# Triangular diagonal score pieces for columns 1 and 2 of the first batch, scored first and completed by DMA transposes

## Chip, cores and metric

One core of one Trainium2 chip. The metric is device microseconds of one execution. The kernel before takes 1192.81 us (median of 3 runs, 1192.8 to 1194.91). On one core the runs have no slow and fast dies to compare.

## The reference, cut to what matters

```python
def _attn_ref(u, v, z):                      # 8 batches, 3008 rows, d_model 256, d_qk 64
    scores = (1.0 / S) * np.matmul(z, z.transpose(0, 2, 1))
    attn = np.maximum(scores, 0.0) ** 2      # symmetric: attn[i, j] == attn[j, i]
    return (u * np.matmul(attn, v)).astype(np.float32)

def _moe_ref(x, w_in, w_out):                # on the 24064 rows of the result
    h = x @ w_in                             # d_ff = 2048
    return ((h * np.cos(h)) @ w_out).astype(np.float32)
```

The attention matrix is symmetric. The kernel uses this: it scores only one side of each pair of pieces and makes the other with a DMA transpose.

## The kernel before

The 3008 rows of a batch are cut into six columns of 512 (the last has 448). A "piece" (b, J, I) holds the squared relu of the scores of key group I against column J, as four blocks of 128 keys. It is made by two score groups, h = 0 and 1: two matmuls on PE, one relu on ScalarE (ACT), one square on VectorE (DVE). 18 buffers hold pieces. In "slot" s = 6 b + J column J is multiplied by v, while the score groups of a later column are put between the matmuls.

```python
    groups = [
        (b, J, I, h)
        for b in range(B)
        for J in range(NC)
        for I in range(0 if b == 0 and J < 3 else J, NC)
        for h in range(2)
    ]
    direct = {(0, 0, 1), (0, 0, 2), (0, 1, 2)}
    # ... cut ...
    def emit_score(later=None):
        b, J, I, h = groups[done_groups[0]]
        done_groups[0] += 1
        cut = I == J and not (b == 0 and J < 3)
        W = 2 * P if cut and h == 0 else width(J)
        # ... cut: two matmuls into e, the second and first half of the rows;
        #     with cut, block n of the diagonal gets (n + 1) * 128 columns only
        nc.scalar.activation(r[:, :, 0:W], e[:, :, 0:W], AF.Relu)
        # ... cut: square r into the piece on VectorE; note the piece for a turn

    def emit_turns(due, more=0):             # on the SP queue, in program order
        # ... cut ...
            if I == J:                       # lower triangle -> upper, three turns
                for rr in range(1, 4):
                    nc.sync.dma_start_transpose(
                        a4[:, 0:rr, rr * P:rr * P + rows],
                        a[0:rows, rr * CW:rr * CW + rr * P],
                    )
            else:                            # one long turn, 16 blocks, to a new piece
                nc.sync.dma_start_transpose(d.rearrange("p (n j) -> p n j", j=P), a)
```

The first three slots have no earlier slot to prepare their pieces, so they are packed by hand:

```python
    def phase_a_first(s, n, extra={}):       # slots 0, 1, 2
        run = 1 if s == 0 else 2
        steps = [                            # dh: the half of the output; k: block of keys
            (dh, k)
            for I in range(0, NC, run)
            for dh in range(2)
            for k in range(4 * I, min(4 * (I + run), last))
        ] + [(2, last)]
        lo, hi = 5 if s == 0 else 2, 42      # n score groups spread over steps lo to hi
        # ...
        for i, (dh, k) in enumerate(steps):
            # ... two value matmuls for step i ...
            for _ in range(at.get(i, 0)):
                emit_score(later=squares if s == 0 and i == lo else None)

    phase_a_first(0, 12, {4: lambda: turn_late(4), 8: lambda: turn_late(5)})
    phase_a_first(1, 12)
    nc.gpsimd.dma_start(w_out16, moe_w_out.rearrange("(k p) f -> p k f", p=P))
    for i in range(2):
        emit_h(0, i)()
    phase_a_first(2, 14)
```

So slots 1 and 2 first read key group 0 at steps 0 to 3, group 1 at steps 4 to 7, and group 2 from step 16.

## Time and profile before

| | before |
|---|---|
| time, median of 3 | 1192.81 us |
| span of the profiled run | 1191.2 us |
| PE (TensorE) busy | 1183.7 us, 99% |
| DVE, ACT, POOL busy | 85%, 67%, 57% |
| mean granted clock | 1.000 |

A busy line gives time, share of the span and instructions of each engine. A timeline line gives start, length, engine, line, operation, and in brackets the idle time ahead of it with what ended it. "PE M L266 <- DVE" in a list of waits means that PE at line 266 waited for DVE.

### The profile page before, as it was taken

Reading aid. Unit: us, or ns where it says so; the run is one execution under the profiler, and the core shown is the slowest. Engines: PE = TensorE matmul, PEld = TensorE weight load, DVE = VectorE, ACT = ScalarE, POOL = GpSimd, SP = SyncE. Lnnn points to the kernel's source line nnn. Section 1 sums busy time; section 2 is a strip of 40 time slices with the busy share of each in tenths; the row PEclk is TensorE's granted clock in tenths of the full one; section 3 lists DMA queues with packets and bytes.
Section 4 is the critical chain, followed back from the end, with each engine's and each line's share of the span. In section 5 each row is a group of like instructions: output and inputs, shape, how many; then the busy total and the mean of one; then the engine's idle time right before and its main releaser. Section 6 shows DMA issues by size and latency. Waiting matters only on the chain.

```text
span 1191.2 us, 29044 instructions
## 1 busy us (share of the span) xinstructions
PE 1183.7 (99%) x11887; PEld 726.8 (61%) x11887; DVE 1011.5 (85%) x1302; ACT 794.9 (67%) x927; POOL 679.0 (57%) x717
## 2 busy tenths in 40 slices
PE   9999999999999999999999999999999999999998
PEld 4556665665566656666566665656666566665566
DVE  6888888889988898888988889888888888888776
ACT  7966676667666676667676676666766666666454
POOL 3286745657466573755647556476555655545452
PEclk9999999999999999999999999999999999999999
DMA  9999999569995799955999469984798837974301
GB/s 160 175 172 158 115 171 130 102 122 104 173 127 101 123 137 166 126 89 103 155 152 130 86 106 158 168 123 70 120 162 152 122 72 120 173 122 84 65 20 54
DMA packets 449142, 148.00 MB, mean 124 GB/s; under 512 B 401264, under 2 KB 432496, under 8 KB 449008
## 3 DMA queue, kind: packets, MB, share of 16 engines
q1 hardware_dynamic: 368464, 112.93, 56.6%
q0 software_dynamic: 80032, 32.78, 27.7%
q8 instruction: 93, 1.52, 0.5%
q10 hardware_dynamic: 512, 0.43, 0.1%
q14 instruction: 41, 0.34, 0.1%
HBM read 66.32 MB, written 24.64 MB: 76 GB/s over the span
## 4 chain that ended last, share of the span: by engine, by line
PE 98%; ACT 1%; DVE 1%; issue 0%; POOL 0%; DVEq 0%; ACTq 0%
PE E L412 27%; PE M L490 23%; PE M L266 20%; PE E L266 19%; PE E L202 6%; PE M L533 1%; ACT r L212 1%; PE M L468 1%; DVE g L423 0%; PE E L673 0%; DVE sm L278 0%; PE E L533 0%; POOL s L441 0%; PE M L696 0%; ACT c L420 0%
## 5 line engine op out<-in xcount | busy, mean ns | idle before, releaser
L420 ACT ACTIVATE c<-E 128x1024 f16<-128x1024 f32 (+1 forms) x384 | 385.7, 1007 | 216.4 <-PE E L412 214.1
L423 DVE SCALAR_TENSOR_TENSOR g<-E,c 128x1024 f16<-128x1024 f32 (+1 forms) x384 | 458.9, 1197 | 62.0 <-ACT c L420 60.9
L212 ACT ACTIVATE r<-E 128x512 f16<-128x512 f32 (+1 forms) x342 | 328.0, 967 | 112.3 <-PE E L202 106.6
L266 PEld LDWEIGHTS <-v 64*128 64x128 f16 x4512 | 245.7, 94 | 229.6 <-issue 18.8
L412 PE MATMUL E<-x,w_in 128*128 128x512 f16 (+1 forms) x1408 | 354.0, 375 | 0.0
L441 POOL TENSOR_TENSOR s<-g 128x512 f16<-128x512 f16 (+1 forms) x184 | 207.8, 1130 | 189.3 <-DVE g L423 139.4
L266 PE MATMUL M<-A,v 64*128 64x512 f16 (+1 forms) x2256 | 283.0, 372 | 0.0
L266 PE MATMUL E<-A,v 64*128 64x512 f16 (+1 forms) x2256 | 278.0, 371 | 0.0
L442 POOL TENSOR_TENSOR g<-g 128x512 f16<-128x512 f16 (+1 forms) x184 | 219.0, 1190 | 14.4
L412 PEld LDWEIGHTS <-w_in 128*128 128x128 f16 x1536 | 133.1, 98 | 108.9 <-issue 19.5
L490 PEld LDWEIGHTS <-g 128*128 128x128 f16 x2816 | 172.5, 98 | 40.8
L217 DVE TENSOR_TENSOR A<-r 128x1024 f16<-128x1024 f16 x240 | 173.2, 734 | 15.1 <-ACT r L212 14.3
L294 POOL TENSOR_TENSOR x<-sm,uT 128x512 f16<-128x512 f32 (+1 forms) x43 | 48.6, 1131 | 223.5 <-DVE sm L278 223.5
L490 PEld LDWEIGHTS <-s 128*128 128x128 f16 x2112 | 129.4, 98 | 32.1 <-DVE s L448 0.5
L202 PE MATMUL E<-zT 64*128 64x512 f16 (+4 forms) x684 | 128.0, 356 | 1.6 <-DVE sm L278 0.7
L448 DVE TENSOR_TENSOR s<-s,g 128x1024 f16<-128x1024 f16 (+1 forms) x92 | 99.7, 1085 | 2.1 <-POOL s L441 2.1
L490 PE MATMUL M<-w_mix,s 128*128 128x128 f16 x1408 | 94.0, 219 | 0.3 <-POOL s L441 0.3
L490 PE MATMUL M<-w_mix,g 128*128 128x128 f16 x1408 | 93.6, 219 | 0.0
L490 PE MATMUL M<-w_out,g 128*128 128x128 f16 x1408 | 93.6, 219 | 0.0
L220 DVE TENSOR_TENSOR A<-r 128x512 f16<-128x512 f16 (+1 forms) x102 | 80.1, 785 | 8.6 <-ACT r L212 7.6
L202 PEld LDWEIGHTS <-zT 64*128 64x128 f16 x684 | 38.7, 94 | 38.4 <-issue 3.8
L450 DVE TENSOR_TENSOR s<-g,s 128x1024 f16<-128x1024 f16 (+1 forms) x92 | 60.6, 661 | 0.0
(58 smaller groups left out, 636.3 us busy)
## 6 DMA issues: line engine op xcount, KB each, us to landing
out_dram<-o SPq DMA_DIRECT2D x87, 256.0 KB, 2.1
v<-in_v_dram POOLq DMA_DIRECT2D x40, 256.0 KB, 11.5
u<-in_u_dram POOLq DMA_DIRECT2D x40, 256.0 KB, 4.5
A<-A SPq DMA_TRANSPOSE x252, 5.3
z<-in_z_dram POOLq DMA_DIRECT2D x14, 192.0 KB, 10.9
z<-in_z_dram POOLq DMA_DIRECT2D x14, 176.0 KB, 6.8
v<-in_v_dram POOLq DMA_DIRECT2D x8, 192.0 KB, 16.1
u<-in_u_dram POOLq DMA_DIRECT2D x8, 192.0 KB, 3.7
```

The source lines that it names most:

```text
L202: nc.tensor.matmul(e[:, t, 0:Wt], zT[rows, k * P:(k + 1) * P], zT[rows, J * CW:J * CW + Wt], start=True, stop=True,)
L212: nc.scalar.activation(r[:, :, 0:W], e[:, :, 0:W], AF.Relu)
L217: nc.vector.tensor_tensor(a4, r4, r4, ALU.mult)
L220: nc.vector.tensor_tensor(a4, r[:, :, 0:W], r[:, :, 0:W], ALU.mult)
L266: nc.tensor.matmul(bank[:, 0:width(J)], vs[b, k // 4][t * H:(t + 1) * H, k % 4, dh * P:(dh + 1) * P], value_rhs(b, J, k, t), start=start, ...
L412: nc.tensor.matmul(e[:, f, 0:W], w_in16[:, k, ft * P:(ft + 1) * P], x[:, k, 0:W], start=(k == 0), stop=(k == 1),)
L420: nc.scalar.activation(c[:, :, 0:W], e[:, :, 0:W], AF.Sin, bias=half_pi, scale=inv_s2)
L423: return lambda: nc.vector.scalar_tensor_tensor(gs[m][:, 2 * i:2 * i + 2, 0:W], e[:, :, 0:W], 1.0, c[:, :, 0:W], ALU.mult, ALU.mult)
L441: nc.gpsimd.tensor_tensor(s1[:, f, 0:n], g[:, f, low], g[:, lower, low], ALU.add)
L442: nc.gpsimd.tensor_tensor(g[:, f, low], g[:, f, up], g[:, f, low], ALU.subtract)
L448: nc.vector.tensor_tensor(s2[:, f, 0:n], s1[:, f, 0:n], g[:, f, up], ALU.subtract)
L490: nc.tensor.matmul(acc[:, k * P:(k + 1) * P], left[:, ft, k * P:(k + 1) * P], right[:, ft, :], start=(ft == 0 and k == 0), stop=(ft == F - ...
```

## The change

The intent: the diagonal pieces (0,1,1) and (0,2,2) are symmetric too, so their upper half need not be scored. This saves work on PE, ACT and DVE in the stretch where ACT has no gaps. The missing blocks come by three transposes each, as everywhere else in the kernel; to give these time to land, the diagonal groups are scored first in their column.

```diff
+    def keys_of(b, J):
+        first = 0 if b == 0 and J < 3 else J
+        return sorted(range(first, NC), key=lambda I: (I != J, I))
+
     groups = [
-        (b, J, I, h)
-        for b in range(B)
-        for J in range(NC)
-        for I in range(0 if b == 0 and J < 3 else J, NC)
-        for h in range(2)
+        (b, J, I, h) for b in range(B) for J in range(NC) for I in keys_of(b, J) for h in range(2)
     ]
@@ emit_score
-        cut = I == J and not (b == 0 and J < 3)
+        cut = I == J and (b > 0 or J > 0)
@@ phase_a_first
                 emit_score(later=squares if s == 0 and i == lo else None)
+                if s < 2:
+                    emit_turns((0, s + 1))
```

## The prediction

> **What bounds the kernel now.** I read the page first: busy shares, then the chain of work that ended last.
>
> ```profile
> PE 1183.7 (99%) x11887; PEld 726.8 (61%) x11887; DVE 1011.5 (85%) x1302; ACT 794.9 (67%) x927; POOL 679.0 (57%) x717
> ...
> PE 98%; ACT 1%; DVE 1%; issue 0%; POOL 0%; DVEq 0%; ACTq 0%
> ```
>
> TensorE (PE) is busy for all but 7.5 us and is 98% of the chain, so nearly anything that keeps PE from its next matmul is paid one for one, and only what shortens PE's own work, or one of its rare waits, is won. An average hides where the change sits, so I went to the place. The diff touches batch 0 alone: two diagonal pieces (0,1,1) and (0,2,2), written (batch, column, key group), scored while the columns ("slots") 0, 1 and 2 are multiplied by v. By the timeline of PE these slots are roughly 9 to 23, 23 to 36 and 38 to 53 us. A table of busy time by windows over 16 to 54 us gives ScalarE (ACT) 36.3 of 38 us, far over its average of 67%, and the timeline of ACT shows slot 0 without a gap:
>
> ```profile
> 13.50 9.60 ACT L212 ACTIVATE r<-E 128x1024 f16<-128x1024 f32 x10
> ```
>
> So in slot 0 ACT sets the pace, PE almost equals it; from 25 us on the chain in order of time is PE again, except around 36 to 41 us, where it passes the copies, cosines and gate of the slot change. That is what makes a triangular cut attractive here. Now PE at the start of slot 1, then at the start of slot 2 (start, length, engine, line, operation; in brackets the idle time before and its releaser):
>
> ```profile
> 23.37 0.40 PE L202 MATMUL E<-zT 64*128 64x512 f16 x2
> 23.58 0.83 PE L266 MATMUL E<-A,v 64*128 64x512 f16 x6
> 25.07 0.39 PE L202 MATMUL E<-zT 64*128 64x512 f16 x2 [0.66 <-DVE sm L278]
> ...
> 39.88 0.39 PE L202 MATMUL E<-zT 64*128 64x512 f16 x2 [0.42 <-DVE g L423]
> 40.09 0.82 PE L266 MATMUL M<-A,v 64*128 64x512 f16 x6
> 41.01 0.39 PE L202 MATMUL E<-zT 64*128 64x512 f16 x2
> 41.22 0.61 PE L266 MATMUL M<-A,v 64*128 64x512 f16 x4
> ```
>
> One "step" of the code is two matmuls of L266; a score group is the two of L202. Each pair's record lasts 0.39 us but the next pair starts 0.22 us later: 0.22 us is its price. Counting steps from a slot's start, 23.58 is steps 3, 4 and 5 of slot 1 and 40.09 is steps 3, 4 and 5 of slot 2; 41.22 is its step 6. Steps 4 to 7 read key group 1. So today group 1 of columns 1 and 2 is read at 23.8 and 40.3 us with no wait for it.
>
> **What the Trainium skill says.** "ScalarE: Activation LUTs", What ACT_TABLE_LOAD costs: an ACTIVATE runs at one element per cycle and lane, 0.833 ns each, over a fixed part. Halving 1024 elements would save 427 ns; the groups by form have both sizes, 1025 and 602 ns, 423 apart: it agrees. "TensorEngine Tiling (Array Packing)", Key Properties: tiles operate independently and in parallel. The 0.22 us per pair with 0.39 us records agrees, and so a pair costs what its wider half costs. "DMA: Bandwidth & Descriptors", Queues, rings and completion order: each DMA engine round-robins between its queues packet by packet. With large packets in one queue and small ones in another, the second gets little. The DMA view of 20 to 22 us agrees:
>
> ```profile
> q0 software_dynamic: 102, 0.42, 103.5%
> ...
> uT<-u SPq DMA_TRANSPOSE x1, 6.0
> A<-A SPq DMA_TRANSPOSE x1, 7.7
> ```
>
> The software queue (packets of 4 KB, the w_in load, issued at 13.8 us, 11.4 us to landing) takes all of the engines' time, and the transpose issued at 20.14 us lands only 6.0 us later.
>
> **The change part by part.**
>
> Removed. For each of the two pieces the first group (h = 0) shrinks from 512 columns to 128 and 256, the second to 384 and 512. PE: the first pair costs half, 0.11 us less, the second nothing less (its wider half is still 512). Two pieces: 0.2 us. ACT: 2 x (1025 - 602) = 0.85 us. VectorE (DVE): 2 x (0.69 - 0.42) = 0.54 us, by the rows of L220 in its timeline. Only the ACT part of piece (0,1,1), 0.42 us, falls where ACT sets the pace, and it would shorten PE's 0.66 us wait at 25.07 us.
>
> Added. Each piece's upper blocks come from three DMA transposes on the SP queue. Their issue on that queue is 1.19 us each (L246: median 1185 ns), and landing takes 2.2/3.9/9.3 us (least, median, most) over the whole run. The built program confirms that step 4 of slot 1 now waits for three DMA semaphores, and step 16 of slot 2 for three others, where it waited for nothing like that.
>
> Moved. The new order scores I = J first. In slot 0 only groups 1 and 0 of column 1 swap, so group 0 is scored last and read at once: its square ends near 23.4 us (23.82 less the 0.42) and step 2 wants it at 23.15: 0.3 us, swallowed by the next wait. In slot 1 the last two scores become (0,2,0) instead of (0,2,1), and (0,2,1) slips into slot 2, after its steps 2 and 5. It is read at steps 4 and 6. This is the part that the intent overlooks.
>
> Stall A, slot 1, step 4. The first group's square ends where it starts today or a little before, 20.2 us (L220 in the timeline of DVE at 20.22), the second's at about 21.7. First turn issued 20.4, second 21.8, third 23.0 to 24.2 us. All compete with w_in, which ends at 25.2. Today's turn of u, 8 blocks, issued 20.14, lands 26.1; these are 6 blocks, the last three issued 3 us later. I take 26.5 us (estimate between 25.5 and 28.5). Step 4 then starts at 26.6, steps 4 and 5 take 0.43, and the score that stands at 25.07 starts at 27.0: 1.9 us later. The 0.66 us wait is inside it, so the 0.42 us of ACT is not won.
>
> Stall B, slot 2. Score at 39.88 (in today's time, its buffer is freed then), ACT 40.30 to 41.33, then square, which DVE can start at 41.36 and end at 42.05 (its row of 0.69 us). Step 4 at 42.1 instead of 40.3. Steps 4 and 5: 42.55. Second score 42.55, ACT 42.97 to 44.0, square to 44.7, step 6 at 44.75 instead of 41.22: 3.5 us later. Nothing else runs on PE in between, as it takes its instructions in order.
>
> Stall C, slot 2, step 16. SP reaches the turns of (0,2,2) behind the long ones, each 2 to 4.4 us of issue from 31 to 43 us today; I get issue at 39.7 to 43.3 and landing near 48. PE wants them at 44.0 + 1.9 + 3.5 = 49.4. Usually no stall, one of 1 to 2 us in one case of four: 0.4 us.
>
> Sum: 1.9 + 3.5 + 0.4 - 0.2 = +5.6 us. 1192.8 + 5.6 = 1198.4 us. After slot 2 PE has no wait until the end (the view of waits from 50 to 1150 us has none for it), so nothing gives it back and everything is only shifted.
>
> **The rivals.** (1) The saving wins: ACT bounds slots 0 to 2, 0.85 us are saved and the turns are hidden: about 1192. For it speaks ACT's 36.3 of 38 us; against it, that from 25 us the chain goes over PE, and that PE in order has no other work at steps 4 and 6. (2) The turns alone hurt, because the scheduling places (0,2,1) early enough in practice: +2, 1194.8. Against it: the program order is fixed and has one step between score and use. (3) The queue is the bound: six more turns delay u's turn and the long ones, and slots 3 to 5, which read those pieces, wait too: +8 to +12, 1201 to 1205. For it: issues of 5.7 us at 43.55, so that queue is backlogged until 60; against it: twelve blocks are less than one long turn of sixteen, while PE itself comes 5 us later. (4) Nothing: 1193, if both stalls fell in PE's idle time; there is only 0.66 + 0.42 us of that.
>
> **Range and chances.** Stall B is arithmetic on measured durations, 3 to 4 us. A depends on one landing time, 0.9 to 4 us. C is 0 to 3. Small ends together give +3.7, large ones about +10, both at once unlikely; and runs of one kernel spread by 2 us. Predicted 1198.4 us, 8 in 10 between 1196 and 1202. Two per cent is 23.9 us, four times the sum: faster 0.005, within 2% 0.98, slower 0.015.
>
> **What would show it.** In the timeline of PE: a wait of about 2.5 us near 24 us released by a DMA that writes A (step A); two waits of 1.5 to 2 us near 42 and 44 us released by DVE L217, one score pair between them (step B); no wait for a DMA near 49 us, or a short one (step C); from slot 3 on the same picture shifted by 5 to 6 us. ACT has two more rows of 602 ns and idle time in both stalls. The prediction is wrong if the turns land by 24 us (A gone), if PE's wait at step 6 is missing (B halved), or if slots 3 to 5 show waits for A by DMA, which would be rival 3.

## More of the kernel before

The lines that carry the argument are in the prediction; one more is needed for later, the clock in 40 slices of the span, in tenths (9 is 90% or more):

```profile
PEclk9999999999999999999999999999999999999999
```

## The result

| | before | changed |
|---|---|---|
| median of 6 runs | 1193.18 us | 1200.66 us |
| lowest to highest | 1192.8 to 1197.65 | 1198.63 to 1202.43 |
| span of the profiled run | 1191.2 us | 1199.5 us |
| mean clock of the profiled run | 1.000 | 0.996 |

The ratio is 1.0054, 95% interval 1.0036 to 1.0072. A ratio here is the mean time of one kernel's fast runs over that of the other's of the same rounds, so it is not quite the ratio of the medians. The changed kernel is slower by 0.5%: within the 2% that count as the same, and inside the predicted range.

The profile after, its busy line and its clock line:

```profile
PE 1187.8 (99%) x11887; PEld 728.0 (61%) x11887; DVE 1010.6 (84%) x1302; ACT 794.1 (66%) x927; POOL 677.8 (57%) x717
...
PEclk9899999999999999999999999999999999999999
```

ACT lost 0.8 us of work and DVE 0.9 us, as the intent wanted. PE has as many matmuls as before, a few of them narrower, and yet is busy 4.1 us longer. The clock line has an 8 in its second slice, 30 to 60 us: matmuls there took longer. The table by windows shows it in numbers (window, its length, then PE, PEld, DVE, ACT, POOL busy with their counts, then granted clock, DMA share, GB/s). First the kernel before, then the changed one:

```profile
23.00:36.00 13.00, 12.34 (x116) 6.36 (x114) 10.13 (x16) 12.26 (x15) 0.75 (x2) 1.00 0.96 169
36.00:53.00 17.00, 16.46 (x137) 8.69 (x132) 14.15 (x21) 16.07 (x19) 1.87 (x3) 1.00 1.29 175
```

```profile
23.00:36.00 13.00, 11.21 (x90) 5.64 (x89) 8.14 (x14) 9.27 (x11) 0.75 (x2) 0.87 0.88 152
36.00:53.00 17.00, 13.08 (x82) 5.27 (x78) 8.77 (x13) 10.28 (x12) 1.87 (x3) 0.80 1.17 156
```

The clock records of the trace have two rates only, 1.00 and 0.50, so clocks of 0.87 and 0.80 mean 2 x 0.13 x 13 = 3.4 us and 2 x 0.20 x 17 = 6.8 us at half speed. The PE timeline of the changed kernel shows where. Slot 1:

```profile
23.49 0.39 PE L266 MATMUL E<-A,v 64*128 64x512 f16 x2 [0.42 <-DVE A L220]
...
25.69 0.91 PE L266 MATMUL E<-A,v 64*128 64x512 f16 x4 [1.37 <-DMA A<-A]
26.35 0.67 PE L202 MATMUL E<-zT 64*128 64x512 f16 x2
26.78 1.10 PE L266 MATMUL E<-A,v 64*128 64x512 f16 x4
...
29.75 0.40 PE L202 MATMUL E<-zT 64*128 64x512 f16 x2
```

Slot 2:

```profile
44.69 0.61 PE L266 MATMUL M<-A,v 64*128 64x512 f16 x4 [1.62 <-DVE A L220]
45.12 0.39 PE L202 MATMUL E<-zT 64*128 64x512 f16 x2
47.36 1.04 PE L266 MATMUL M<-A,v 64*128 64x512 f16 x4 [1.85 <-DVE A L220]
48.16 0.66 PE L266 MATMUL E<-A,v 64*128 64x512 f16 x2
...
52.85 0.77 PE L266 MATMUL M<-A,v 64*128 64x512 f16 x4
53.45 0.39 PE L202 MATMUL E<-zT 64*128 64x512 f16 x2
```

The waits are where the prediction put them: step 2 of slot 1 (0.42, for the square of group 0, scored last), step 4 of slot 1 (1.37, for the turns), steps 4 and 6 of slot 2 (1.62 and 1.85, for the two squares of (0,2,1)). What it does not have is what follows two of them: a pair of matmuls whose record is 0.39 us takes 0.66 us, and the next pair starts 0.43 us later and not 0.22.

The account, from start times of the same instruction in both traces (a record's idle time leaves out the 0.17 us tail of the pair before it, so the lost time between starts is a little more than the bracket says):

| part | us |
|---|---|
| slot 1 starts at 22.46 instead of 22.72 | -0.26 |
| slot 1, waits: 0.60 and 1.55 lost, against 0.84 before | +1.31 |
| slot 1, half clock: 11 pairs from 25.69 to 29.75, 4.06 us instead of 2.37 | +1.69 |
| rest of slot 1, with one narrower pair (34.92) | -0.16 |
| slot 2, waits: 1.80 and 2.02 lost, less a small wait of 0.27 before (ahead of 41.01) | +3.55 |
| slot 2, half clock: 15 pairs from 47.36 to 53.45, 6.09 us instead of 3.24 | +2.85 |
| rest of slot 2, where a small wait before (0.15, ahead of 48.02) is gone | -0.22 |
| sum | +8.76 |

The first product with w_in after slot 2 (L412, L414 in the changed kernel) starts at 61.65 instead of 52.88 us, 8.77 later; the last matmuls of the program start at 1193.73 instead of 1184.96, again 8.77. All is lost by the end of slot 2 and nothing comes back while PE runs. The spans differ by 8.3; the 0.5 between lies after the last matmuls began, and I did not follow it.

The six runs of the changed kernel fit this: clock 0.996 with 1201.28, 1201.2 and 1202.43 us, 0.997 with 1200.13, 0.998 with 1199.37 and 1198.63. 0.002 of mean clock is 2.4 us of time, so they seem to differ mostly in how long the half clock lasted; only the first of them left a trace.

"TensorE: Matmul & The Clock Gate" in the Trainium skill, What's actually happening, tells of a gate that halves PE's clock after an idle window of about 3.4 us and restores it after a busy one, the window running freely. Stretches of 3.4 and 6.8 us at half pace agree with one and two windows. The silences do not fill such a window, though: 1.37 and 1.85 us; how much silence it takes here is counted under e5. I had not used that page in the prediction.

### The profile page after: what moved, and what is told of

It is laid out like the page before. It is cut to its first block, busy times and chain, and to the rows that moved or that the text cites. A ratio compares the mean times of both kernels' runs of the same rounds, so it can differ in the third digit from the quotient of the medians.

```text
span 1199.5 us, 29057 instructions
## 1 busy us (share of the span) xinstructions
PE 1187.8 (99%) x11887; PEld 728.0 (61%) x11887; DVE 1010.6 (84%) x1302; ACT 794.1 (66%) x927; POOL 677.8 (57%) x717
## 5 line engine op out<-in xcount | busy, mean ns | idle before, releaser
L414 PE MATMUL E<-x,w_in 128*128 128x512 f16 (+1 forms) x1408 | 354.1, 375 | 0.0
L266 PE MATMUL E<-A,v 64*128 64x512 f16 (+1 forms) x2256 | 281.2, 374 | 1.8 <-DMA A<-A 1.4
L444 POOL TENSOR_TENSOR g<-g 128x512 f16<-128x512 f16 (+1 forms) x184 | 218.7, 1189 | 14.4
L414 PEld LDWEIGHTS <-w_in 128*128 128x128 f16 x1536 | 133.0, 98 | 109.0 <-issue 19.5
L217 DVE TENSOR_TENSOR A<-r 128x1024 f16<-128x1024 f16 x240 | 172.2, 729 | 22.5 <-ACT r L212 21.7
L294 POOL TENSOR_TENSOR x<-sm,uT 128x512 f16<-128x512 f32 (+1 forms) x43 | 48.5, 1129 | 223.8 <-DVE sm L278 223.8
L220 DVE TENSOR_TENSOR A<-r 128x512 f16<-128x512 f16 (+1 forms) x102 | 80.1, 785 | 11.0 <-ACT r L212 10.3
```

Of the source, the lines that this page charges most:

```text
L217: nc.vector.tensor_tensor(a4, r4, r4, ALU.mult)
L220: nc.vector.tensor_tensor(a4, r[:, :, 0:W], r[:, :, 0:W], ALU.mult)
L266: nc.tensor.matmul(bank[:, 0:width(J)], vs[b, k // 4][t * H:(t + 1) * H, k % 4, dh * P:(dh + 1) * P], value_rhs(b, J, k, t), start=start, ...
L414: nc.tensor.matmul(e[:, f, 0:W], w_in16[:, k, ft * P:(ft + 1) * P], x[:, k, 0:W], start=(k == 0), stop=(k == 1),)
L444: nc.gpsimd.tensor_tensor(g[:, f, low], g[:, f, up], g[:, f, low], ALU.subtract)
```

## The experiments

Two theories. Theory 1: the loss is PE waits (for the turns, and for (0,2,1), scored one step before its use) plus half clock after such silence. Rivals: the turns and their queue cause all of it; or the long matmul records come from contention and not from the clock; or the cut is a gain and the order alone is to blame. Eleven kernels ran, all gave correct results.

| run | median us | ratio to before (95%) | clock, profiled run |
|---|---|---|---|
| e1_order_only | 1198.60 | 1.0037 (1.0017 to 1.0057) | 0.997 |
| e2_cut_only | 1212.87 | 1.0156 (1.0138 to 1.0173) | 0.993 |
| e3_fillers | 1200.75 | 1.0059 (1.0034 to 1.0084) | 1.000 |
| e4_scores_14_12 | 1201.09 | 1.0056 (1.0033 to 1.0078) | 0.997 |
| e5_order_fillers | 1196.38 | 1.0029 (1.0012 to 1.0046) | 0.999 |
| e6_column1_only | 1195.57 | 1.0021 (1.0006 to 1.0036) | 0.998 |
| e7_column1_late_read | 1195.43 | 1.0022 (1.0007 to 1.0037) | 1.000 |
| e8_order_late_read | 1193.84 | 1.0007 (0.9992 to 1.0021) | 0.999 |
| e9_late_read_early_wout | 1194.44 | 1.0013 (1.0001 to 1.0026) | 0.999 |
| e10_before_early_wout | 1192.97 | 0.9998 (0.9986 to 1.0011) | 0.999 |
| e11_change_late_read | 1200.88 | 1.0068 (1.0052 to 1.0083) | 0.998 |

The kernel before had medians of 1193.4 (with e1 to e4), 1193.13 (e5 to e8) and 1193.09 us (e9 to e11), at a clock of 0.999 or 1.000 always. In the profiled runs of e5, e8, e9 and e10 the only slow stretch begins after the last matmul and reaches into the last 1.3 to 1.7 us of the span, so their 0.999 means no slow matmul. The three groups of rounds ran on three chips; each run is best compared with the kernel before of its own rounds.

### One part at a time: e1_order_only and e2_cut_only

e1, new order, but nothing cut and no turns:

```diff
-        cut = I == J and (b > 0 or J > 0)
+        cut = I == J and not (b == 0 and J < 3)
@@ phase_a_first
-                if s < 2:
-                    emit_turns((0, s + 1))
```

> New order of the score groups, but full diagonal pieces and no turns by DMA. Theory 1 (two stalls of TensorE, each followed by a stretch at half clock): the wait on a DMA in slot 1 is gone, the two waits of slot 2 stay at 1.6 and 1.85 us, and the half-speed stretch after them stays; 3.5 us of waits plus 0 to 3.4 us of slow clock make 1196.5 to 1200 us. Rival (the six turns and the DMA queue cause it all): 1193 us.

Measured 1198.60 us. PE's timeline in slot 2 has the same two waits to the last digit, with no DMA in it, and the same slow pairs after the second:

```profile
41.89 0.61 PE L266 MATMUL M<-A,v 64*128 64x512 f16 x4 [1.62 <-DVE A L220]
42.32 0.41 PE L202 MATMUL E<-zT 64*128 64x512 f16 x2
44.58 1.04 PE L266 MATMUL M<-A,v 64*128 64x512 f16 x4 [1.85 <-DVE A L220]
45.38 0.66 PE L266 MATMUL E<-A,v 64*128 64x512 f16 x2
```

The queue cannot be the whole cause: order alone costs 5.2 us by the medians.

e2, cut and turns, old order:

```diff
-        return sorted(range(first, NC), key=lambda I: (I != J, I))
+        return range(first, NC)
@@ phase_a_first
-                if s < 2:
-                    emit_turns((0, s + 1))
+                emit_turns((0, s + 1 if s < 2 else 2))
```

> Triangular cut and turns, but the groups in the old order. Theory 1: the turns of piece (0,1,1) are issued about 2 us later, so step 4 of slot 1 waits about 3 us; those of (0,2,2) come only in slot 2 and step 16 waits 4 to 6 us; slow clock after each: 1203 to 1207 us, worse than the whole change. Rival (order alone is to blame, the cut is a gain): at or under 1193 us.

Measured 1212.87 us: the direction is as expected, the size is not. PE's waits of this run:

```profile
PE M L266 <- DMA A<-A: 11.5, 1, 11.5
PE E L266 <- DMA A<-A: 5.7, 1, 5.7
```

I had expected 4 to 6 and 3 us. The SP queue works in program order: in this run five long turns hold it from 35.24 to 53.9 us, and the turns of (0,2,2) are issued only at 54.00. The rival that blames the order alone falls: the cut without the order is much worse, so the new order was needed for the turns.

### Is it the clock? e3_fillers and e5_order_fillers

e3 is the changed kernel with idle matmuls ahead of three of the waits (their results are overwritten):

```diff
+        spare = M if s == 1 else pair
         for i, (dh, k) in enumerate(steps):
+            for f in range({(1, 4): 6, (2, 4): 7, (2, 6): 8}.get((s, i), 0)):
+                nc.tensor.matmul(spare[1], warm[:, 0:P], warm, start=True, stop=True)
```

> The changed kernel with 6, 7 and 8 idle matmuls put just before the three waits, into a PSUM bank not in use there, sized a little shorter than the waits. Theory 1: the waits stay where they are, but TensorE never falls silent, the half-speed stretches vanish (mean clock 1.000) and about 4.3 us of the 8 come back: 1196 to 1197.5 us. Rival (long records after the waits come from memory or DMA contention, not from the clock): nothing comes back, 1200 to 1201.5 us, clock still 0.996.

The profiled run took 1198.97 us, the median is 1200.75: the expectation of the time failed, and the median alone lies where the rival put it. Of the clock the expectation held, in both windows of the profiled run:

```profile
23.00:36.00 13.00, 12.58 (x112) 5.65 (x111) 9.05 (x15) 10.80 (x13) 0.75 (x2) 1.00 1.00 164
36.00:53.00 17.00, 14.46 (x101) 5.88 (x99) 10.09 (x15) 10.63 (x13) 1.88 (x3) 1.00 1.26 182
```

and PE's records are 0.39 us again after each filled wait. But a new wait stands at step 16 of slot 2, where the prediction had its stall C:

```profile
50.75 0.61 PE L266 MATMUL M<-A,v 64*128 64x512 f16 x4 [2.06 <-DMA A<-A]
```

In the changed kernel PE came to this step at 52.85 us, 0.9 us after the last turn of (0,2,2) had landed (issued at 43.02, 8.9 us to landing). Without the slow clock it comes by about 48.5, and waits until 50.7. So nearly half of what the clock gives back is taken by the turns. The four runs spread from 1198.97 to 1204.3; the slowest again has a clock of 0.997.

e5 does the same (7 and 8 idle matmuls, slot 2) to the order-only kernel, which has no such turns.

> The order-only kernel with 7 and 8 idle matmuls before its two waits in slot 2. No turns by DMA exist here, so nothing behind them can open up. Theory 1 (half clock after silence): mean clock 1.000, both waits of 3.5 us together stay as time, the 2.9 us of slow clock come back: 1195.5 to 1196.5 us against 1198.6 without the idle matmuls. Rival (the long matmul records have another cause): 1198 to 1199 us.

Measured 1196.38 us (1196.35 to 1196.77), 2.2 us under e1 by the medians, or 1.95 when each is taken against the kernel before of its own rounds. The profiled run has no slow stretch while matmuls run, and the two steps (x4) whose records took 1.04 us after e1's second wait take 0.61, behind the idle matmuls of L378:

```profile
42.65 1.90 PE L378 MATMUL E<-s 128*128 128x512 f16 x8
44.56 0.61 PE L266 MATMUL M<-A,v 64*128 64x512 f16 x4
44.99 0.39 PE L266 MATMUL E<-A,v 64*128 64x512 f16 x2
```

In e1 the 15 pairs from 44.58 us take 5.59 us, in e5 the same 15 from 44.56 take 3.24: 2.35 us came back, by the same instructions and with the same dependences. The long records are the clock, and silence of PE is what brings it about. What stays, 3.3 us over the kernel before, is the two waits.

The traces also show how much silence it takes. In each run the stretches of full and of half clock begin and end on one grid of 3.41 us. I counted PE's idle time (no matmul record) in every window of this grid, in all 13 profiled runs, some 4500 windows:

| clock in a window | PE idle in it | clock in the next window |
|---|---|---|
| full | 1.61 us or less | full, without exception |
| full | 1.70 us or more | half, without exception |
| half | 0.64 us or less | full, without exception |
| half | 1.01 us or more | half, without exception |

The windows before the falls have 1.79 and 2.46 us of idle time in the changed kernel, 2.05 in e1 and 1.70 in e6. A wait of 2.20 us in e4 had no such effect because a border of the grid, at 24.87 us, cut it: the windows on its two sides have 1.06 (with the 0.42 us wait) and 1.55 us. So it is the silence inside one window that counts, in several pieces or in one, and where the grid lies differs from run to run.

### Can the waits be moved? e4_scores_14_12

```diff
-    phase_a_first(1, 12)
+    phase_a_first(1, 14)
-    phase_a_first(2, 14)
+    phase_a_first(2, 12)
```

> The changed kernel with 14 score groups in slot 1 and 12 in slot 2, so that (0,2,1) is scored in slot 1 again. Theory 1: both waits of slot 2 vanish with their slow stretch, the DMA wait of slot 1 stays: +1.1 us of wait and about +1.5 us of slow clock over the kernel before, 1195 to 1196.5 us. Rival (ScalarE cannot take two more groups in slot 1, or pieces run short): slot 1 grows by 2 us and the time stays at 1197 or above.

Measured 1201.09 us; the rival is nearer. The waits of steps 4 and 6 are gone and slot 2 runs at full pace, up to its end. There the list of waits between 45 and 65 us has:

```profile
DVE A L217 <- DMA A<-A: 8.0, 2, 6.9
...
ACT r L212 <- DVE A L217: 5.4, 1, 5.4
PE E L414 <- ACT r L212: 4.6, 1, 4.6
```

The scores now run two groups ahead, and a square of (0,3,4) wants a buffer that a long turn still has to read; that turn, issued at 48.76 behind the others in the SP queue, lands at 58.21. DVE waits 6.9 us, ACT for DVE, PE for ACT. It was the buffers and the queue, not ScalarE's pace. The wait for the turns in slot 1 was 2.20 us here, and no slow clock followed it; the 4.6 us wait of PE was followed by half clock until 65.8 us.

### Each place alone: e6_column1_only, e7_column1_late_read, e8_order_late_read

e6 cuts and reorders column 1 only:

```diff
-        return sorted(range(first, NC), key=lambda I: (I != J, I))
+        return sorted(range(first, NC), key=lambda I: (I != J or J == 2, I))
-        cut = I == J and (b > 0 or J > 0)
+        cut = I == J and (b > 0 or J not in (0, 2))
```

> Cut, turns and new order for column 1 alone; column 2 as before. Theory 1 (the costs are separable by place): only the DMA wait of slot 1 is left, 1.1 to 1.9 us after what the kernel before waits there, plus 0 or 1.7 us of slow clock: 1194.5 to 1197 us. Rival (the extra transposes on the queue also disturb later slots): 1198 us or more.

Measured 1195.57 us. The profiled run has the 0.42 us wait, one of 1.28 us for the turns, and then 3.4 us at half clock, as in the whole change; slot 2 is as before. The costs of the two columns stand apart by place.

e7 is e6 with a later reading of group 1 in slot 1:

```diff
-        run = 1 if s == 0 else 2
+        run = 1 if s < 2 else 2
```

> As the kernel with column 1 alone, but slot 1 multiplies key group 0 for both halves of the output first, so group 1 is read from step 8 and not from step 4, 0.86 us later. Theory 1: the wait for the turns shrinks by 0.9 us to under 1 us, no slow clock: 1193 to 1194.5 us, level with the kernel before; the 0.4 us that ScalarE saves can at best make it 1193. Rival (the wait just moves to another place): as with column 1 alone, 1194.5 to 1197 us.

Measured 1195.43 us, above the range that I gave, and yet the mechanism worked: the wait for the turns is 0.30 us, no clock is lost, and the product with w_in after slot 2 starts at 52.72 us, 0.16 before that of the kernel before. Then:

```profile
PE M L535 <- DMA w_out<-in_moe_w_out_dram: 2.2, 1, 2.2
```

The load of w_out, issued at 38.93, lands 17.9 us later; in the kernel before it is issued at 39.09 and lands after 14.4 us, 1.1 us ahead of its first use. A margin that no view of the page had shown was used up. That the extra turns did this, as the expectation of e9 takes for granted, is not shown: in e7 they have all landed by 25.4 us; the same load takes 16.4 us in e5, which has no extra turns, and 12.2 and 13.4 us in e3 and e11, which have six. Why it was late here stays open.

e8 is the order-only kernel with the late reading in slot 2:

```diff
-        run = 1 if s == 0 else 2
+        run = 2 if s == 1 else 1
```

> The order-only kernel, but slot 2 multiplies key group 0 for both halves first, so (0,2,1) is read from steps 8 and 10 and not from 4 and 6. Theory 1 (the cost is the single step between score and use): the two waits of 3.5 us shrink to 0.7 us together and the clock stays full: 1193.5 to 1194.5 us. Rival (the reordering costs in another way, for example through buffers): 1196 us or more.

Measured 1193.84 us, all four runs within 0.45 us, as expected. The 3.5 us of waits become 0.6:

```profile
PE M L266 <- DVE A L220: 0.6, 2, 0.3
```

So the cost of the order was the single step between score and use; what else it may cost is within the noise (ratio 1.0007, 0.9992 to 1.0021). Reading the piece four steps later hides nearly all of it.

### Is there a version that wins? e9, e10 and e11

e9 is e7 with the load of w_out moved:

```diff
+    nc.gpsimd.dma_start(w_out16, moe_w_out.rearrange("(k p) f -> p k f", p=P))
     phase_a_first(1, 12)
-    nc.gpsimd.dma_start(w_out16, moe_w_out.rearrange("(k p) f -> p k f", p=P))
```

> The kernel with column 1 alone and the late read, and the load of w_out issued before slot 1 instead of after it. Theory 1: the 2.2 us wait for w_out that the extra transposes brought about is gone, nothing else waits, and slot 2 ends 0.2 us earlier than in the kernel before: 1192.7 to 1193.3 us, level or ahead by 0.2 us. Rival: the w_out packets now fall on the turns of (0,1,1) and the wait for these comes back, 1 to 3 us: 1194 to 1196 us.

The median is 1194.44 us (1192.8 to 1196.96). The profiled run has no wait for w_out any more, and the wait for the turns is 0.28 us; a wait of 0.8 us for the sums of slot 2 has come instead. The median lies where the rival put it, but not for the rival's reason. The best run, 1192.8, is what was hoped for, but three of five lie above 1194 at full clock. Where those lose their time is open: a trace exists of one run only.

e10 moves the same load in the kernel before:

> The kernel before with the load of w_out issued before slot 1, as a control. Theory 1: the load has about 1 us in hand in the profiled run of the kernel before, so the median does not move, 1192.8 to 1193.3 us, and its slow outliers at full clock (1196 us) become rarer. Rival (early w_out is worth something in itself): under 1192.3 us.

Measured 1192.97 us, ratio 0.9998: no effect, as expected. Whether outliers become rarer cannot be told from five runs; one of them took 1194.21.

e11 is the whole change with the late reading in both slots (`run = 1`):

> The whole change with the late read in slots 1 and 2. Theory 1: the wait on DMA in slot 1 falls to 0.3 us and those on VectorE in slot 2 to 0.6 us, as in the single tests; but PE then comes to step 16 of slot 2 some 5 us earlier, at about 45 us, while the turns of (0,2,2) land near 46 to 49: a wait on DMA of 2 to 4 us there, followed by a slow stretch in some runs, 1196 to 1199 us. Rival (the turns come in time): 1193.5 to 1194.5 us, level with the kernel before.

Measured 1200.88 us, no better than the change itself and above the range that I gave. The single waits shrank as in the tests before (0.90 for the turns in slot 1, 0.28 and 0.31 for the squares). PE reaches step 16 of slot 2 at 45.7 us, and then:

```profile
45.47 0.40 PE L266 MATMUL E<-A,v 64*128 64x512 f16 x2
50.26 1.03 PE L266 MATMUL M<-A,v 64*128 64x512 f16 x4 [4.39 <-DMA A<-A]
51.07 0.65 PE L202 MATMUL E<-zT 64*128 64x512 f16 x2
```

In e3 the step went on at 50.75, here at 50.26: the last turn of (0,2,2) lands at 50.1 us here, 50.6 in e3 and 52.0 in the changed kernel, although PE comes at 45.7, 48.5 and 52.85; the turns are issued behind the long ones (39.63 to 44.2 us here, 40.50 to 44.3 in the changed kernel). After this wait the clock is at half for 3.4 us, as the long records show. In the change itself this third wait was there all along, hidden under the first two and the slow clock.

## Why the prediction was right

The time, 1200.66 us against 1198.4, lay in the range; the two stalls are where the prediction put them and have the causes that it named. The sum came out too small because one term was missing. That the time stayed in the range without this term of 4.5 us is in part luck: stalls A and C were smaller than counted. The number alone would not have told the account from rival (3), which began at 1201; the traces did.

- The savings: said 0.2 us on PE, 0.85 on ACT, 0.54 on DVE. A narrower pair came out 0.15 us cheaper (the next starts 0.07 us later, not 0.22), 0.3 for both; ACT's busy time fell by 0.8 and DVE's by 0.9. (The 427 ns in the prediction are an estimate from the page; the sum used the trace's 423.) The claim that ACT's part would not be won is right in its result; the 0.26 us by which slot 1 starts earlier went into the wait behind it.
- Stall A: said 1.9 us, with the turns in at 26.5. They let PE go at 25.69, and the waits cost 1.3 us more than before. The load of w_in landed at 24.2 in this run, 1.0 us before the time that the estimate used. e6 shows this stall alone, e7 shows it nearly vanish. The DMA view of 20 to 22 us, shown in the prediction after the page on DMA, does not show queues taking turns: no packet of the hardware queue moved before 23 us, although a transpose was issued at 20.14. No run here tests that rule, and stall A rests on the landing time alone.
- Stall B: said 3.5 us; 3.55 in the trace (the releaser is the square of L220, not of L217 as the signs had it). The chain score, relu, square, read was measured durations put in a row. e1 and e8 confirm it: it is there with order alone, and goes when the read is four steps later.
- Stall C: said 0.4 on average and usually none. None appeared in the profiled run, but for a reason that the prediction did not have: the half clock had made PE late, so that it came 0.9 us after the landing. e3 and e11 show 2.1 and 4.4 us of it. The estimate of the landing, near 48 us, was 2 to 4 us too early.
- The step that failed: "Sum". It counted waits as the only price of a wait. Half clock after two of the waits cost 1.69 + 2.85 = 4.5 us, nearly as much as the waits themselves. A mean clock under 1.000 was not among the signs that the prediction named. e5 against e1 shows the effect with only the idle matmuls added. The large ends of the range were added up to about 10 us; they give 10.8.
- The rivals: (1), the saving wins, is refuted by the result, and no version here hides all the turns: e11, which removes most of the other waits, still waits 4.4 us for those of (0,2,2). (2), the turns alone hurt, is refuted by e1. (3), the queue is the bound, is wrong for slots 3 to 5, where PE has no new wait, but right about what blocks a repair: e4 and e11 ran into the queue, and e7 into a late load whose cause is open. (4) is refuted by the result.

## What to carry to other kernels

When an engine is 99% busy and its instructions stand in a fixed order, count the steps between a value's making and its use after every reordering; a cheaper piece that is due one step later costs the whole chain of the engines between. Price a silence of TensorE at its length plus a possible stretch at half clock (here whenever 1.70 us or more of one 3.41 us window were idle), and look at the granted clock by windows before believing that longer matmuls have another cause. And when a wait is removed, look up when the next input lands: waits in a row hide each other, so that fixing the first may move the time not at all.

## What the Trainium skill lacked or had wrong

- "TensorE: Matmul & The Clock Gate", Why this matters for your kernels, advises no PE gaps over about 3 us. Here 1.28 us (e6) and 1.37 us (the change), each shortly after one of 0.42, and 1.85 after one of 1.62 were followed by half clock, while gaps of 2.20 (e4) and 2.06 us (e3) were not. What decided it, in every window of every trace, was the idle time within one window of a fixed grid of 3.41 us: 1.70 us, about half a window, was enough, and 1.61 was not. The page's own remark that the window runs freely fits this; that half a window suffices it does not say.
- Nor does it say how busy a window must be to restore the clock: 0.64 us idle still did, 1.01 us did not.
- The same page does not say that idle matmuls ahead of a wait in mid-kernel keep the clock: no slow stretch in the profiled runs of e3 and e5, and 2.35 us of matmul time back in e5.
- "DMA: Bandwidth & Descriptors" has no time to landing of transposes between buffers of the SBUF beside other traffic: from 2.2 us (the shortest diagonal turn) to 19.3 us (the longest long one) in the kernel before, and 1.7 to 11.5 us of issue time for a turn of 16 blocks, which delays what stands behind it in the SP queue (e2: five of them from 35.24 to 53.9 us, the next turns at 54.00).
